# Low parts last in the divided sixth product, its block copies in layer one's last product, row statistics behind weight loads

## The chip, the cores and the metric

The kernel runs on one core of a Trainium2 chip. The metric is device time in microseconds (us) from the start of the launch to its end. Engines are named as the profile names them: PE is the matrix engine (TensorE; PEld are its weight loads), DVE is VectorE, ACT is ScalarE, POOL is GpSimd, SP is the sync engine, which only issues transfers. Transfers (DMAs) are issued from two queues: SP's (hardware, q1) and POOL's (software, q0).

## The reference

Two identical layers, each an attention without softmax and then a gated block that mixes over the sequence. Sequence S = 2048, width D = 512, 32 heads of 16, F = 1792, FH = 896. All is float32.

```python
x = x + A(layernorm(x));  x = x + B(layernorm(x));  x = x + A(layernorm(x));  x = x + B(layernorm(x))

def A(x):                      # phi(t) = (t + 1 if t > 0 else exp(t)) + 1e-6
    q, k, v = split_heads(x @ wqkv)
    kv, z = sum_s phi(k) v,  sum_s phi(k)
    return merge_heads(phi(q) kv / (phi(q) z + 1e-6)) @ wo

def B(x):
    z = gelu(x @ w_in)                        # [S, 1792]
    z1, z2 = z[:, :896], layernorm(z[:, 896:])
    g = w_sp @ z2 + b_sp[:, None]             # [S, S] x [S, 896]
    return (z1 * g) @ w_out
```

## The kernel before

Every matrix product in float32 is made from three products of rounded parts: an operand is split in a high part `h` (a copy by ACT) and a low part `l` (what is left, a subtraction by DVE), and PE adds h·h, h·l and l·h in one bank. So each tile of a weight costs one ACT pass, one DVE pass and three matmuls of 512 columns.

The program is written out in order for each engine; tile pools fix which buffer a tile gets and semaphores what it waits for. Within an engine's queue nothing overtakes, so the order of rows is the order of issue.

Each layer runs four stages. **P1** goes over the 16 row tiles of x (steps s = 1 to 18): layer norm, a transpose by way of DRAM (`xt`, loaded back by SP and turned by DVE at L448), the K and Q products, phi, and sums over K. In it SP also loads the weights of later stages, and `FSums` sums and splits parts of `w_in`. **The transition** forms the key-value state. **P2** makes the attention's output and z = gelu(x w_in); in layer two, `epair` makes z for two row tiles at a time by a seven-product scheme, and the row statistics of z are made from sums: `e3m` the mean on POOL, then a square with a running sum on ACT (L1084), then three POOL operations (L1086 to L1088) that give the factors with which `e4` normalises. `tail` is P2's last piece: `T[5]`, `T[6]`, `T[7]`, `T[4]` are its products with weights `w1s` and `w` which `wfetch` loads into pages through POOL (L205); `fmul` (L1145 to L1147) makes their matmuls.

**P4** multiplies by w_sp, also with seven products of block sums, in the order P2, P1, P6, P7, P4, P5, P3; a product has 8 steps k. Some of the seven are divided once more into seven products r of two steps each (`DIVIDED`: P2 and P4 in layer one, P2, P4 and P5 in layer two; the sixth product in this order is P5). Before a step's matmuls SP loads the step's raw block (`fetch1`), and `wsp` splits it: high part on ACT (L1678), low part on DVE (L1681). Some low parts (`KEPT`: P7, and of P5 the steps r = 1, 2, 4) are stored in DRAM by SP in layer one (`lowP7`, `lowP5`, L1686), and layer two loads them through POOL (L1684) instead of making them again. `mm_div` makes the 12 matmuls of a divided step through `acc` (L1889 h·high, L1890 h·low, L1891 l·high), `evac_div` adds the finished banks into the result's units, `gate` multiplies by z1.

The divided products need sums of two blocks of w_sp (or of `s1`, the block sums that layer one stores). They are built in DRAM by `halve(n)`: the first pieces are plain copies by SP (L1551), the others accumulating transfers by POOL (L1555), which add a second block into the copy; each moves 512 KB. `PARTS` says in which step of layer one's P4 which piece n runs, and a line in P1 runs the rest in layer two. The eight copies for P5 are n = 16 to 23, its eight adds n = 24 to 31.

Of the kernel before, what the change touches and what calls it, by code (L numbers as in the profile page):

```python
# [15 lines left out]
P = 128  # L16
# [3 lines left out]
NT = S // P  # L20
# [76 lines left out]
KEPT = ("P7", "P5")  # L97
# [13 lines left out]
FILL = {7: 3, 9: 3, 11: 3, 13: 3, 15: 3}  # L111
WADD = {2: 0, 4: 1, 6: 2}
PARTS = {("P1", 4 + k): k for k in range(4)} | {("P6", k): 4 + k for k in range(8)}
PARTS |= {("P7", k): 12 + k for k in range(4)}
LEFT = 4
SPN = 3
LOAD2 = (9, 10, 11, 14)
# [35 lines left out]
def mixer_kernel(ctx: ExitStack, tc: tile.TileContext, x_in, wqkv, wo_d, win1_d, win2_d, wsp_d, bsp_d, wout_d,  # L153
                 ident_d, mask_d, out_d):
    nc = tc.nc
# [7 lines left out]
    pages = Slots(main, "pg", 22)  # L163
    quads = Slots(main, "qd", 6)
# [288 lines left out]
    class P1:  # L453
# [185 lines left out]
        def run(self, sums):  # L639
            side = deque([self.win2] * NF)  # L640
            ND = NT - DEFER
            for s in range(1, NT + 2):
                for i in self.ahead(s, LEAD - 1, 3):
                    self.loadx(i)
                for i in self.ahead(s, LEAD + 1, 1):
                    self.turn.load(i)
                if 2 <= s < NT:
                    self.T_high(s)
                if s == 1:
                    if not self.kb:  # L650
                        self.K(0)
                    self.K(1)
                elif 2 < s <= NT:
                    self.K(s - 1)
                for i in self.ahead(s, LEAD, 2):
                    self.ln_a(i)
                if 2 <= s < NT:
                    self.T_low(s)
                if s <= NT:
                    self.K_phi(s - 1)  # L660
                if s <= ND:
                    self.Q(s - 1)
                if s == NT + 1:
                    self.late()
                if s <= NT:
                    self.xsplit(s - 1)
                    self.K_split(s - 1)
                for i in self.ahead(s, LEAD, 2):
                    self.ln_b(i)
                if s <= ND:  # L670
                    self.Q_phi(s - 1)
                if s >= 2:
                    self.Gmm(s - 2)
                if s == NT + 1:
                    self.late_phi()
                if self.L == 0:
                    if s == 2:
                        sums.slots = Sheets(bigs, 2)
                    if 2 <= s < 10:
                        sums.tick(s < 9)  # L680
                    if s == 10:
                        sums.store()
                    sums.store2()
                    if s in LOAD2:
                        sums.load2(pages if s > 12 else sums.slots)
                if s == 11:
                    self.wv = quads.get([P, 4, 512])
                    nc.sync.dma_start(self.wv, wqkv[:, 1024:1536].rearrange("(c p) f -> p c f", p=P))
                if s == 14:
                    self.wo = quads.get([P, 4, 512])  # L690
                    nc.sync.dma_start(self.wo, wo_d.rearrange("(c p) f -> p c f", p=P))
                if s in range(3,NT-1):
                    self.turn.pre(s + 1)
                if self.L == 0:
                    sums.add2(1, POOL2.get(s, 0))
                    sums.add2(0, DVE2.get(s, 0))
                if self.L:
                    if s > 1:
                        sums.halve(14 + s, None)
                    if s in WADD:  # L700
                        if not WADD[s]:
                            self.fsums = FSums()
                        self.fsums.load(WADD[s])
                    if s - 1 in WADD:
                        self.fsums.sums(WADD[s - 1])
                    if s - 2 in WADD:
                        self.fsums.split(WADD[s - 2])
                        if WADD[s - 2] == 2:
                            self.fsums.close()
                    if s <= 4:  # L710
                        self.win2.load(2)
                    else:
                        self.win2.piece()
                    if s == NT - 1:
                        self.win2.sums()
                    if s == NT:
                        self.win2.last()
                    continue
                if s > 3 and side:
                    side.popleft().piece()  # L720
                if s > 2 and side:
                    side[0].fetch()
# [104 lines left out]
    class P2:  # L827
# [167 lines left out]
        def epair(self, i, *between):  # L995

            V, A = nc.vector, nc.scalar.activation
            todo = deque(between)
            z = [ztag(i + k, [P, FH], f"z{self.L}") for k in range(2)]
            lo, hi = slice(0, HF), slice(HF, FH)  # L1000
            z0, z1 = ((t[:, lo], t[:, hi]) for t in z)

            def gelu(o, b):
                k, j = (o is not z0[0] and o is not z0[1]) * 1, (o is z0[1] or o is z1[1]) * 1
                self.mark = A(o, b, AF.Gelu_apprx_tanh, accum_out=self.acc(i + k)[:, j:j + 1])

            def other():
                if todo:
                    todo.popleft()()

            u = banks.get([P, HF])
            self.emul(i, 1, u, True, False)
            y = banks.get([P, HF])
            A(y, u, AF.Copy)
            v = banks.get([P, HF])
            self.emul(i, 5, v, True, True)
            c = z1[1]
            A(c, v, AF.Copy)
            banks.put(v)
            self.fout()  # L1020
            self.emul(i, 6, y, False, False)
            d = banks.get([P, HF])
            A(d, y, AF.Copy)
            V.tensor_add(y, y, c)
            other()
            self.emul(i, 2, u, False, True)
            gelu(z0[0], u)
            banks.put(u)
            self.emul(i, 7, d, False, False)
            V.tensor_add(c, d, c)  # L1030
            other()
            self.emul(i, 3, y, False, True)
            gelu(z0[1], y)
            banks.put(y)
            other()
            self.emul(i, 4, d, False, True)
            gelu(z1[0], d)
            gelu(z1[1], c)
            banks.put(d)
            pages.put(self.S.pop(i)[0][1])  # L1040
            while todo:
                other()
            self.e3m(i)
            self.e3m(i + 1)

        def e(self, i):
            n, k = divmod(i, 4)
# [25 lines left out]
                a = self.zacc[i] if a is None else a  # L1073
                nc.gpsimd.tensor_scalar(a[:, 2:3], a[:, 0:1], a[:, 1:2], -1.0 / FH, op0=OP.add, op1=OP.mult)

        def e3(self, i):
            if not self.L:
                self.zms[i] = stats(ztile[i], 2)
                return
            a = self.zacc.pop(i)  # L1080
            self.e3m(i, a)
            nm, v, rs, nb = (a[:, k:k + 1] for k in range(2, 6))
            t = pages.get([P, FH], mybir.dt.bfloat16)
            nc.scalar.activation(t, ztile[i], AF.Square, bias=nm, accum_out=v)  # L1084
            pages.put(t)
            nc.gpsimd.tensor_scalar(rs, v, 1.0 / FH, LN_EPS, op0=OP.mult, op1=OP.add)  # L1086
            nc.gpsimd.tensor_tensor(rs, rs, mhalf, op=OP.pow)
            nc.gpsimd.tensor_scalar(nb, nm, rs, None, op0=OP.mult)  # L1088
            self.zms[i] = None, rs, nb
# [111 lines left out]
        def tail(self):  # L1201
            V, A = nc.vector, nc.scalar.activation
            h, l = (t.bitcast(F32) for t in self.xT[3])
# [17 lines left out]
            for f in range(3):  # L1221
                ws.append(self.ws.popleft())
                v = banks.get(PAGE)
# [5 lines left out]
            for f in range(3):  # L1229
                y = self.y[f]  # L1230
                self.fmul(y, [t[:, 256:512] for t in ws[f]], self.T[6], False, False)
                pages.put(*ws[f])
                self.wfetch()
                d.append(banks.whole(PAGE))
                A(d[f], y, AF.Copy)
                V.tensor_add(y, y, c[f])
# [15 lines left out]
            x = [t[:, 2:4] for t in self.xT[3]]  # L1252
# [8 lines left out]
            for i in (NT - 2, NT - 1):  # L1261
                _, rs, nb = self.zms.pop(i)
                V.tensor_scalar(ztile[i], ztile[i], rs, nb, op0=OP.mult, op1=OP.add)
            for f in range(3):
                w = self.ws.popleft()
# [120 lines left out]
        def run2(self):  # L1386
            late = self.p1
            for s in range(1, NT + 3):
# [19 lines left out]
                else:  # L1408
# [44 lines left out]
                    if pair:  # L1453
# [22 lines left out]
                        elif s > NT:  # L1476
# [6 lines left out]
                            def late3():  # L1483
                                self.raw(1)
                                quads.put(*self.xT.pop(2))
                                self.T2()
                                self.e3(NT - 4)
                                self.e3(NT - 3)

                            self.epair(s - 4, late4, late3)  # L1490
                        else:
# [119 lines left out]
    class P4:  # L1611
# [79 lines left out]

        def kept(self, g):
            p, k = self.steps[g]
            if p not in KEPT or p == "P3" and k > 4:
                return None
            if p not in self.div:
                t = self.sums.lows[p][:, k]
# [104 lines left out]
        def mm_div(self, g, p, m):  # L1802
# [3 lines left out]
            name = "F" if r in (5, 3) else "X" if r in (1, 2) else "Y"  # L1806
            if q == 0 and r in (1, 5):
                self.bank[name] = [banks.get(PAGE) for _ in range(2)]
            if q == 0 and r == 6:
                pass  # L1810
            for i in range(2):
                for f in range(2):
                    self.acc(self.bank[name][f], h[:, i], l[:, i], slice(f * P, (f + 1) * P), w, i,
# [565 lines left out]
```

## Time and profile before

| | us |
|---|---|
| median of 3 runs | 1353.09 (1351.85 to 1355.10) |
| profiled execution | 1351.78 |
| its span | 1350.0 |
| PE busy | 1340.0 |
| DVE busy | 1037.7 |
| ACT busy | 726.3 |
| POOL busy | 463.8 |

The granted clock was 1.000 over the span. Rows of the timeline give start, duration, engine, line, operation, output and inputs, and in brackets the idle time before the row and what ended it. The names are those of the program: `pg`, `qd`, `bg` are pages of 512, 2048 and 3584 floats a partition, `bank` is a PE accumulator. A matmul's duration there is longer than the distance to the next, since they are pipelined: what counts is the distance from start to start. Layer two's P1 lies from about 680 to 815 us, its P2 to 1015, its P4 behind that.

### The profile page before, as it was taken

To read this page: it belongs to the slowest core of one execution; us is meant where nothing else is said; L and a number is where in the kernel's file an instruction comes from. 1 tells how busy PE (TensorE), PEld (TensorE's weight loads), DVE (VectorE), ACT (ScalarE), POOL (GpSimd) and SP (SyncE) were. 2 spreads that over 40 slices of the span, in tenths; PEclk is the share of its full clock that TensorE was granted. 3 is DMA by queue.
4 is the path that set the end of the run, shared out by engine and by line. 5 is a ranking of instruction groups with operands and counts; after the bars stand their busy time and mean duration, and the time that the engine had idled before them with its cause. 6 is when DMAs were issued, how large, how long until landed. Compare 5 with 4: busy or idle time off the path is not lost.

```text
span 1350.0 us, 19217 instructions
## 1 busy us (share of the span) xinstructions
PE 1340.0 (99%) x6540; PEld 1141.3 (85%) x6540; DVE 1037.7 (77%) x1658; ACT 726.3 (54%) x1219; POOL 463.8 (34%) x613
## 2 busy tenths in 40 slices
PE   9999999999999999999999999999999999999998
PEld 7888888888888888889988888888888888877898
DVE  7679877763797689897866877777689757889885
ACT  5774544334643255445667755556687333656454
POOL 3765765544122300301435453545450023022021
PEclk9999999999999999999999999999999999999999
DMA  5898477878877996843678783678767447479343
GB/s 183 277 311 281 164 264 252 289 262 263 296 241 266 299 292 208 291 164 64 152 192 287 208 199 94 204 249 252 235 195 252 143 171 264 155 242 315 106 78 64
DMA packets 174515, 294.50 MB, mean 218 GB/s; under 512 B 14544, under 2 KB 53968, under 8 KB 174160
## 3 DMA queue, kind: packets, MB, share of 16 engines
q1 hardware_dynamic: 155280, 253.67, 55.9%
q0 software_dynamic: 19136, 39.59, 13.4%
q8 instruction: 51, 0.84, 0.2%
q14 instruction: 48, 0.39, 0.1%
HBM read 206.18 MB, written 103.81 MB: 230 GB/s over the span
## 4 chain that ended last, share of the span: by engine, by line
PE 86%; DVE 4%; DMA 4%; issue 3%; ACT 1%; POOL 1%; SPq 0%; DVEq 0%; POOLq 0%; ACTq 0%
PE bank L1890 12%; PE bank L1891 12%; PE bank L1889 12%; PE bank L230 11%; PE bank L228 11%; PE bank L229 11%; PE bank L2087 3%; PE bank L2088 3%; PE bank L2089 3%; DMA qd<-lowP 1%; PE bank L988 1%; PE bank L987 1%; PE bank L986 1%; DMA pg<-xt 1%; PE bank L2101 1%
## 5 line engine op out<-in xcount | busy, mean ns | idle before, releaser
L1890 PE MATMUL bank<-qd,pg 128*128 128x512 f32 x760 | 296.1, 390 | 2.5 <-DMA qd<-lowP 1.7
L1889 PE MATMUL bank<-qd,pg 128*128 128x512 f32 x760 | 295.7, 389 | 0.0
L1891 PE MATMUL bank<-qd,pg 128*128 128x512 f32 x760 | 295.7, 389 | 0.0
L1678 ACT ACTIVATE qd<-qd 128x1024 fp32r<-128x1024 f32 x142 | 149.6, 1054 | 143.0 <-PE bank L1891 115.5
L1681 DVE TENSOR_TENSOR qd<-qd,qd 128x1024 fp32r<-128x1024 f32 x128 | 162.1, 1268 | 60.4 <-ACT qd L1678 60.4
L230 PE MATMUL bank<-qd,pg 128*128 128x512 f32 x448 | 174.8, 390 | 0.0
L1890 PEld LDWEIGHTS bank<-qd,pg 128*128 128x128 f32 x760 | 142.7, 188 | 33.3 <-DMA qd<-lowP 2.8
L1889 PEld LDWEIGHTS bank<-qd,pg 128*128 128x128 f32 x760 | 142.7, 188 | 29.7 <-ACT qd L1678 0.2
L1891 PEld LDWEIGHTS bank<-qd,pg 128*128 128x128 f32 x760 | 142.7, 188 | 29.5
L1930 POOL TENSOR_TENSOR bg<-bg,pg 128x512 f32<-128x512 f32 x28 | 47.9, 1710 | 213.6 <-DVE bg L1944 99.6
L228 PE MATMUL bank<-qd,pg 128*128 128x512 f32 x308 | 120.3, 391 | 0.3 <-DVE pg L217 0.3
L229 PE MATMUL bank<-qd,pg 128*128 128x512 f32 x308 | 120.0, 390 | 0.0
L230 PEld LDWEIGHTS bank<-qd,pg 128*128 128x128 f32 x448 | 84.1, 188 | 18.6 <-DVE pg L217 1.0
L363 POOL TENSOR_SCALAR rs<-mv 128x1 f32<-128x1 f32 x80 | 24.6, 308 | 197.4 <-DVE mv L361 188.0
L372 ACT ACTIVATE pg<-pg,nb,rs 128x512 f32<-128x512 f32 x52 | 42.1, 812 | 85.0 <-POOL nb L366 78.6
L1587 POOL TENSOR_TENSOR pg<-pg,pg 128x512 f32<-128x512 f32 x48 | 67.4, 1403 | 58.4 <-DMA pg<-in_wsp_dram 56.5
L214 ACT ACTIVATE pg<-pg 128x512 fp32r<-128x512 f32 x85 | 53.0, 624 | 63.1 <-DVE pg L448 18.2
L2089 PE MATMUL bank<-wo,qd 128*128 128x256 f32 x288 | 81.4, 283 | 0.0
L2087 PE MATMUL bank<-wo,qd 128*128 128x256 f32 x276 | 78.1, 283 | 0.0
L2088 PE MATMUL bank<-wo,qd 128*128 128x256 f32 x276 | 78.0, 283 | 0.0
L228 PEld LDWEIGHTS bank<-qd,pg 128*128 128x128 f32 x308 | 57.8, 188 | 12.6 <-DVE pg L217 0.7
L229 PEld LDWEIGHTS bank<-qd,pg 128*128 128x128 f32 x308 | 57.8, 188 | 12.1 <-DVE qd L217 0.3
(270 smaller groups left out, 3242.2 us busy)
## 6 DMA issues: line engine op xcount, KB each, us to landing
qd<-s SPq DMA_DIRECT2D x62, 512.0 KB, 4.3
qd<-in_wsp_dram SPq DMA_DIRECT2D x40, 512.0 KB, 4.0
qd<-hP SPq DMA_DIRECT2D x40, 512.0 KB, 4.6
pg<-z SPq DMA_DIRECT2D x56, 256.0 KB, 3.9
pg<-in_wsp_dram SPq DMA_DIRECT2D x52, 256.0 KB, 4.3
s<-pg SPq DMA_DIRECT2D x48, 256.0 KB, 3.7
z<-pg SPq DMA_DIRECT2D x40, 256.0 KB, 3.1
pg<-w POOLq DMA_DIRECT2D x38, 256.0 KB, 4.6
```

The lines of the kernel that those rows point to most:

```text
L228: nc.tensor.matmul(out, ah, bh, start=start, stop=False)
L229: nc.tensor.matmul(out, ah, bl, start=False, stop=False)
L230: nc.tensor.matmul(out, al, bh, start=False, stop=stop)
L1587: nc.gpsimd.tensor_tensor(t, a, b, op=OP.add)
L1678: self.mark = nc.scalar.activation(w[:, 0], r, AF.Copy)
L1681: nc.vector.tensor_sub(w[:, 1], r, w[:, 0].bitcast(F32))
L1889: m(out, h[:, o], w[:, 0, j, :], start=start, stop=False, skip_group_check=True)
L1890: m(out, h[:, o], w[:, 1, j, :], start=False, stop=False, skip_group_check=True)
L1891: m(out, l[:, o], w[:, 0, j, :], start=False, stop=stop, skip_group_check=True)
L2087: m(out, A, x, start=start and f == 0, stop=False, skip_group_check=True)
L2088: m(out, A, y, start=False, stop=False, skip_group_check=True)
L2089: m(out, B, x, start=False, stop=stop and f == 2, skip_group_check=True)
```

## The change

Four edits. (1) In layer two, the steps of P5 whose low part is loaded make their eight matmuls with the high weight part first and the four with the loaded low part last; there are 12 as before. (2) The eight copies for P5 (n = 16 to 23) run in layer one's P3 (the last product) instead of in steps 2 to 9 of layer two's P1, and the adds (n = 24 to 31) run at P1's even steps 2 to 16 instead of at steps 10 to 17. (3) P7's steps 6 and 7 aren't kept: layer one doesn't store their low parts, layer two makes them on DVE. (The condition that stood there before, on P3, never applied.) (4) In the tail, the row statistics of tiles NT-4 and NT-3 (`e3r`) and the means of NT-2 and NT-1 (`e3m`) come later among the loads of `wfetch`; the squares stay where they were.

```diff
@@
-PARTS |= {("P7", k): 12 + k for k in range(4)}
+PARTS |= {("P7", k): 12 + k for k in range(4)} | {("P3", k): 16 + k for k in range(8)}
@@ P1, layer two
-                    if s > 1:
-                        sums.halve(14 + s, None)
+                    if s % 2 == 0:
+                        sums.halve(23 + s // 2, None)
@@ epair
-            self.e3m(i)
-            self.e3m(i + 1)
+            if i < NT - 2:
+                self.e3m(i)
+                self.e3m(i + 1)
@@
-        def e3(self, i):
+        def e3(self, i, rest=True):
...
-            a = self.zacc.pop(i)
+            a = self.zacc[i]
             self.e3m(i, a)
...
+            if rest:
+                self.e3r(i)
+
+        def e3r(self, i):
+
+            a = self.zacc.pop(i)
+            nm, v, rs, nb = (a[:, k:k + 1] for k in range(2, 6))
             nc.gpsimd.tensor_scalar(rs, v, 1.0 / FH, LN_EPS, op0=OP.mult, op1=OP.add)
@@ tail
                 self.fmul(y, [t[:, 256:512] for t in ws[f]], self.T[6], False, False)
                 pages.put(*ws[f])
                 self.wfetch()
+                if f == 0:
+                    self.e3m(NT - 2)
+                    self.e3m(NT - 1)
+                if f == 1:
+                    self.e3r(NT - 4)
+                    self.e3r(NT - 3)
@@ run2, late3
-                                self.e3(NT - 4)
-                                self.e3(NT - 3)
+                                self.e3(NT - 4, False)
+                                self.e3(NT - 3, False)
@@ kept
-            if p not in KEPT or p == "P3" and k > 4:
+            if p not in KEPT or p == "P7" and k > 5:
@@ mm_div
+            if self.L and self.kept(g) is not None:
+                M = nc.tensor.matmul
+                for x in range(2):
+                    for i in range(2):
+                        for f in range(2):
+                            o, b = slice(f * P, (f + 1) * P), self.bank[name][f]
+                            if x:
+                                M(b, h[:, i, o], w[:, 1, i, :], start=False, stop=r in (2, 4) and q == 1 and i == 1,
+                                  skip_group_check=True)
+                            else:
+                                M(b, h[:, i, o], w[:, 0, i, :], start=r == 1 and q == 0 and i == 0, stop=False,
+                                  skip_group_check=True)
+                                M(b, l[:, i, o], w[:, 0, i, :], start=False, stop=False, skip_group_check=True)
+                pages.put(h, l)
+                quads.put(w)
+                return
```

PE, the first step of P5 in layer two, before. `qd5_179` holds the step's weights, high and low, `pg0` the high part of z, `pg10` its low part; L1890 is the matmul with the loaded low part.

```order
L1889 MATMUL bank5_367_11948<-qd5_179_11897,pg0_1130_11851 128x512
L1890 MATMUL bank5_367_11948<-qd5_179_11897,pg0_1130_11851 128x512
L1891 MATMUL bank5_367_11948<-qd5_179_11897,pg10_1131_11852 128x512
L1889 MATMUL bank1_368_11949<-qd5_179_11897,pg0_1130_11851 128x512
L1890 MATMUL bank1_368_11949<-qd5_179_11897,pg0_1130_11851 128x512
L1891 MATMUL bank1_368_11949<-qd5_179_11897,pg10_1131_11852 128x512
```

The same step after, from its third pair on: L1833 and L1835 are the products with the high weight part, L1830 those with the loaded low part.

```order
L1833 MATMUL bank5_367_11946<-qd5_179_11895,pg0_1130_11849 128x512
L1835 MATMUL bank5_367_11946<-qd5_179_11895,pg10_1131_11850 128x512
L1833 MATMUL bank1_368_11947<-qd5_179_11895,pg0_1130_11849 128x512
L1835 MATMUL bank1_368_11947<-qd5_179_11895,pg10_1131_11850 128x512
L1830 MATMUL bank5_367_11946<-qd5_179_11895,pg0_1130_11849 128x512
L1830 MATMUL bank1_368_11947<-qd5_179_11895,pg0_1130_11849 128x512
```

The first matmul that reads the low part was the step's second and is its ninth.

POOL in layer two's tail, before, from the last two statistics of tile NT-3 on: `acc` are the sums and factors of a row tile, `w1s` and `w` the weights that `wfetch` loads.

```order
L1086 TENSOR_SCALAR acc<-acc 128x1
L1087 TENSOR_TENSOR acc<-acc,mhalf 128x1
L1088 TENSOR_SCALAR acc<-acc 128x1
L1074 TENSOR_SCALAR acc<-acc 128x1 x2
L205 DMA pg_981_10265<-w1s_1_0_119 128x512
L205 DMA pg_982_10267<-w1s_1_1_120 128x512
L205 DMA pg_984_10303<-w_3_0_101 128x256
L205 DMA pg_985_10305<-w_3_1_102 128x256
L205 DMA pg_986_10316<-w_4_0_103 128x256
L205 DMA pg_987_10318<-w_4_1_104 128x256
L205 DMA pg_988_10329<-w_5_0_105 128x256
L205 DMA pg_989_10331<-w_5_1_106 128x256
```

And after (L1075 is the mean, L1094 to L1096 are the statistics of NT-4):

```order
L205 DMA pg_981_10255<-w1s_1_0_119 128x512
L205 DMA pg_982_10257<-w1s_1_1_120 128x512
L205 DMA pg_984_10293<-w_3_0_101 128x256
L205 DMA pg_985_10295<-w_3_1_102 128x256
L1075 TENSOR_SCALAR acc<-acc 128x1 x2
L205 DMA pg_986_10308<-w_4_0_103 128x256
L205 DMA pg_987_10310<-w_4_1_104 128x256
L1094 TENSOR_SCALAR acc<-acc 128x1
L1095 TENSOR_TENSOR acc<-acc,mhalf 128x1
L1096 TENSOR_SCALAR acc<-acc 128x1
```

The same three rows for NT-3 follow, and only then `w_5_0_105` and `w_5_1_106`. The two `w1s` loads and the first two `w` loads moved ahead of all eight row operations; the last two `w` loads stand behind all of them.

SP in layer two's P1, step 2, before: `xt` is the transposed x, `hP` the piece for P5, `in_win` parts of w_in.

```order
L419 DMA xt_4_7071<-pg_667_7069 128x4x128
L1551 DMA hP_1_0_164<-s_145 16x8192
L734 DMA qd_108_7094<-in_win_dram 128x512 x2
L302 DMA bg_15_7021<-in_win_dram 128x512 x2
L196 DMA pg_668_7100<-x_5_84 128x512
L196 DMA pg_669_7102<-xt_4_7071 128x512
```

POOL in the same step, after: the add that takes the copy's step stands behind the sum over K (L542).

```order
L363 TENSOR_SCALAR rs<-mv 128x1
L364 TENSOR_TENSOR rs<-rs,mhalf 128x1
L366 TENSOR_SCALAR nb<-mv,rs 128x1
L542 TENSOR_TENSOR pg_652_6994<-pg_652_6994,pg_662_7049 128x512
L1569 DMA hP_1_0_164<-s_145 128x1024
```

The copy left SP's queue, and the add came into POOL's, at the even steps; at the odd steps nothing took the copy's place.

More of the change, by code (lines that the diff above doesn't have):

```diff
@@ L1808, in mm_div @@
                 self.bank[name] = [banks.get(PAGE) for _ in range(2)]
-            if q == 0 and r == 6:
-                pass
+            if self.L and self.kept(g) is not None:
[14 more added lines that the diff above has]
+                return
             for i in range(2):
```

## The prediction

> **What bounds the kernel now.** I read the page's busy shares first, then the table of what TensorE (PE) waited for, then the timeline around each of its waits.
>
> ```profile
> PE 1340.0 (99%) x6540; PEld 1141.3 (85%) x6540; DVE 1037.7 (77%) x1658; ACT 726.3 (54%) x1219; POOL 463.8 (34%) x613
> ...
> PE bank L617 <- DVE pg L612: 2.3, 1, 2.3
> PE bank L1890 <- DMA qd<-lowP: 1.7, 2, 0.9
> PE bank L1147 <- DMA pg<-w1s: 0.9, 1, 0.9
> PE bank L1890 <- DVE qd L1681: 0.8, 1, 0.8
> PE bank L228 <- DVE pg L217: 0.3, 1, 0.3
> ```
>
> PE is busy 1340.0 of 1350.0 us. The diff leaves every matmul in the program, so only PE's waits can move the end. The list is short. The first line is the program's start and stays. The second and third name the loads that this change makes less urgent or issues earlier. The last two are a weight split in layer one and a step of layer two's first stage (P1).
>
> ```profile
> 1203.29 0.39 PE L1891 MATMUL bank<-qd,pg 128*128 128x512 f32 x1
> 1203.52 0.39 PE L1889 MATMUL bank<-qd,pg 128*128 128x512 f32 x1
> 1204.82 0.50 PE L1890 MATMUL bank<-qd,pg 128*128 128x512 f32 x1 [0.91 <-DMA qd<-lowP]
> 1205.15 0.40 PE L1891 MATMUL bank<-qd,pg 128*128 128x512 f32 x1
> ...
> 1237.45 0.39 PE L1889 MATMUL bank<-qd,pg 128*128 128x512 f32 x1
> 1238.66 0.50 PE L1890 MATMUL bank<-qd,pg 128*128 128x512 f32 x1 [0.83 <-DMA qd<-lowP]
> ...
> 1005.35 0.39 PE L1146 MATMUL bank<-bg,pg 128*128 128x512 f32 x1
> 1006.60 0.50 PE L1147 MATMUL bank<-bg,pg 128*128 128x512 f32 x1 [0.86 <-DMA pg<-w1s]
> ...
> 755.14 0.39 PE L230 MATMUL bank<-pg,pg 128*128 128x512 f32 x1
> 755.78 0.50 PE L228 MATMUL bank<-qd,pg 128*128 128x512 f32 x1 [0.25 <-DVE pg L217]
> ```
>
> The reader should measure from start to start. Undisturbed matmuls start 0.23 us apart (1203.29 to 1203.52). At 1203.52 the next one comes 1.30 later, so 1.07 are lost; the one behind it comes 0.33 later, 0.10 more. The first wait on lowP thus costs 1.17, the second 0.98 + 0.10 = 1.08, the wait on w1s 1.02 + 0.10 = 1.12, the one at 755 0.41 + 0.10 = 0.51.
>
> **The sixth product's matmuls (mm_div).** Each of the 6 divided steps keeps its 12 matmuls. The loaded low part was an operand of the second; now it is one of the ninth. That is 7 x 0.227 = 1.59 us of grace, more than the 1.07 and 0.98 that the loads were late. The grace is lost if the load starts later too, so its issue matters:
>
> ```profile
> 1197.02 0.72 POOL L1684 DMA_DIRECT2D qd<-lowP  x1 [3.18 <-DMA qd<-hP]
> ...
> 1229.75 0.72 POOL L1684 DMA_DIRECT2D qd<-lowP  x1 [1.96 <-PE bank L1891]
> ```
>
> The second issue waits for a matmul that frees its buffer, the first for the raw block of the same buffer chain. Both move with PE and don't lag behind it, and the 1.59 hold in relation to PE. Margins of 0.5 and 0.6 us stay. Gain: 1.17 + 1.08 = 2.25; bounds 1.1 (one load again too late) and 2.3. The price is that the bank's last value for the first half comes 2 matmuls (0.45) later for the evacuation on DVE, on which PE doesn't wait in the list above.
>
> **The row statistics in the tail.** On POOL six statistics and two means stood ahead of eight weight loads:
>
> ```profile
> 992.97 0.73 POOL L1086 TENSOR_SCALAR acc<-acc 128x1 f32<-128x1 f32 x1 [2.78 <-ACT pg L1084]
> ...
> 998.78 1.43 POOL L1074 TENSOR_SCALAR acc<-acc 128x1 f32<-128x1 f32 x2
> 1000.15 1.18 POOL L205 DMA_DIRECT2D pg<-w1s  x2
> ...
> 1005.31 0.19 POOL L1086 TENSOR_SCALAR acc<-acc 128x1 f32<-128x1 f32 x1 [0.75 <-ACT pg L1084]
> 1005.58 0.57 POOL L1087 TENSOR_TENSOR acc<-acc,mhalf 128x1 f32<-128x1 f32 x1
> 1006.25 0.30 POOL L1088 TENSOR_SCALAR acc<-acc 128x1 f32<-128x1 f32 x1
> ```
>
> The last load that PE wants at 1005.35 went out at 1000.77 and landed at 1006.56, 5.8 later. With nothing ahead but a page that comes free about 994 (with the second of the squares, of which the row at 992.97 waited for the first), it goes out some 6 us earlier and lands near 1000. The 1.12 go. What is late next are the loads w_105 and w_106, now behind the six statistics:
>
> ```profile
> 998.63 1.29 DVE L1216 TENSOR_TENSOR qd<-qd,pg 128x512 f32<-128x512 f32 x2
> ...
> 1014.48 0.39 PE L1145 MATMUL bank<-bg,pg 128*128 128x512 f32 x1
> ...
> DMA to landing us min/median/max: 2.9/5.0/9.7
> ```
>
> The load w_101 can't go before its page is read at 999.93 (the end of the DVE row). Two loads, two means (1.43) and two loads follow, 0.55 each: 1003.6. Then come six statistics, 2 x (0.19 + 0.57 + 0.30 and gaps) = 2.6 at the fast price, 5.8 at the price of 992.97 to 998.78. So w_105 starts at 1006.2 to 1009.4, and with the tile's median landing (the last row) is there at 1011.2 to 1014.4. PE wants it at 1014.48, by then 1.12 earlier: 1013.36. From 2.2 early to 1.0 late. I take 0, since the DVE work beside POOL after 1003 is that of the fast rows. Gain of the part 1.12; bounds 0.1 and 1.12. The means and statistics themselves are read over 4 us later.
>
> On the length of such a load the Trainium skill, "DMA: Bandwidth & Descriptors", section "Anatomy of one DMA — SWDGE (gpsimd) path", fits 2.0 us plus bytes by 436 GB/s. For 256 KB that is an estimate of 2.6 us, by which w_105 could not be late in any case; the row above has a minimum of 2.9 and a median of 5.0, so the trace decides for the longer one.
>
> **The block copies and adds.** Eight 512 KB copies leave the SP queue of layer two's P1 for layer one's last product. There DMA has room, and PE's operands there were over 4 us early:
>
> ```profile
> 587.00:594.00 7.00, 7.00 (x33) 5.79 (x32) 6.97 (x13) 4.32 (x8) 0.00 (x0) 1.00 0.71 246
> ```
>
> Cost there 0 (the DMA share, next to last, is 0.71 in the fullest of four such windows); if that cover were gone, a copy costs what it does below. In P1 the copies of steps 2 to 9 go, and accumulating adds, which lay at steps 10 to 17, take steps 2, 4, 6 and 8, with the rest at even steps to 16. Their price:
>
> ```profile
> q1 hardware_dynamic: 155280, 253.67, 55.9%
> q0 software_dynamic: 19136, 39.59, 13.4%
> ...
> 730.00:745.00 15.00, 15.00 (x68) 12.43 (x67) 10.87 (x18) 11.38 (x22) 7.20 (x10) 1.00 0.87 293
> ...
> 742.40 0.73 DVE L448 STREAM_TRANSPOSE bank<-pg 128x512 f32<-128x512 f32 x1 [1.17 <-DMA pg<-xt]
> ...
> 747.49 0.63 ACT L535 ACTIVATE pg<-pg 128x512 fp32r<-128x512 f32 x1 [2.05 <-DVE pg L524]
> ...
> 750.71 0.69 DVE L524 SCALAR_TENSOR_TENSOR z_q<-bank,z_q 128x512 f32<-128x512 f32 x1 [1.86 <-ACT z_q L521]
> ```
>
> From the queues' shares, SP's transfers cost 0.559 x 1350 / 253.67 = 2.97 us a MB, 1.56 for 512 KB; POOL's 4.57 a MB, 2.40. An add for a copy is 0.84 us more of a full burst in each even step, and one copy less in each odd step, where the engines come to rest anyway. At step 6 that decides: the load of xt that VectorE waits for at 742.40 ends such a burst, and from there DVE, ACT (747.49) and DVE (750.71) hand on without slack to the wait at 755. So 0.84 later there is 0.84 later on PE. At step 2 and 4 PE is over 2 us ahead. The adds' issue on POOL (0.9 each) lies in idle time of 3 to 5 us. I take +0.85: the price of the nearest rows. Bounds: -0.5 (the adds don't delay xt, and the wait at 755 goes too) and +1.7 (step 8 pays as well).
>
> A rule speaks against this part: the Trainium skill, "DMA: Bandwidth & Descriptors", section "Issuing engines are not separate DMA queues", says that transfers started by POOL and SP run on the same 16 engines and interleave, so POOL's queue is no way around SP's burst. By that rule the part is a loss as taken here; if the queues were independent it would be 0 to -0.5, and the sum 0.85 to 1.35 lower (rival 1). The share of 0.87 in a window with both agrees with the rule.
>
> **Product P7's two low parts.** Layer one drops two 512 KB stores, layer two drops two loads of POOL and splits on DVE instead:
>
> ```profile
> L1681 DVE TENSOR_TENSOR qd<-qd,qd x128: 1209/1221/2334, 340.9 to 1260.5; 128x1024 fp32r<-128x1024 f32 x128
> ...
> 1140.00:1160.00 20.00, 20.00 (x89) 16.54 (x89) 13.48 (x30) 8.92 (x14) 1.43 (x2) 1.00 0.73 238
> ...
> 499.61 3.67 DVE L1949 TENSOR_TENSOR bg<-pg,bank 128x512 f32<-128x512 f32 x6
> ```
>
> Two splits of 1.22 us lie on a DVE that is busy 13.48 of 20 there. The first also waits for ACT, which holds the DVE queue about 3 us; what stands behind is used 7 us later. Cost 0, and if that cover were gone up to 2. In layer one the wait of 0.8 on L1681 ends a run of DVE work (six evacuations, 3.67 us) whose first weight landed ahead of the stores: -0.05, with -1.0 as the end.
>
> **Sum.** -2.25 - 1.12 - 0.05 + 0.85 = -2.6. Against the profiled execution (1351.78, span 1350.0 and 1.8 around it) 1349.2; that execution was 1.31 below the median of three, 1353.09, from which I forecast 1350.5. No change within 0.2% is 1350.4 to 1355.8 here, about what a measurement of this kernel can tell.
>
> **The rivals.** (1) The adds are hidden, or layer one's wait goes as well. For it: the odd steps lose a copy, and two stores leave SP's queue. Against it: the full burst at 742.40, and the DVE run at 499.61. Time: 1353.09 - 3.4 - 0.5 to -1.0 = 1348.7 to 1349.2.
>
> (2) The grace isn't enough in one place: one lowP load late by another 0.6, or w_105 behind slow statistics. Then 1.0 to 1.2 come back: 1351.5 to 1351.7. For it the longest landing of 9.7; against it the margins above. If the reordering did nothing at all, both lowP waits would stay: 1352.7.
>
> (3) Slower: the adds jam the first half of P1. Landing times, for the adds and then for the copies, were:
>
> ```profile
> DMA to landing us min/median/max: 5.0/8.3/9.6
> ...
> DMA to landing us min/median/max: 4.0/5.6/10.1
> ```
>
> If an add delays xt not by 0.84 but by the 2.7 us between those medians, steps 6 and 8 each pay 2.7, step 4 the 0.6 above its 2.1 of slack: +6.0, the sum +2.6, 1355.7. From 2.8 us an add on, it is slower by over 0.2%; at 4 us it is 2 x 4 + 1.9 - 3.4 = +6.5, 1359.6. For it: adds read and write what copies only write. Against it: in all of POOL's traffic 512 KB took 2.40 us.
>
> **How the numbers follow.** Forecast 0.40 (own range 1349.8 to 1351.4, half of it faster by over 0.2%); rival 1 0.25; rival 2 0.20; rival 3 0.15, of which 0.13 beyond +0.2%. Faster: 0.20 + 0.25 = 0.45. Slower 0.13. Same: 0.20 + 0.20 + 0.02 = 0.42. The range, 1348.4 to 1354.6, leaves the far part of rival 3 and the low end of rival 1 with layer one's wait in full.
>
> **What would show it.** In the profile after, PE's waits should have no line for lowP and none for w1s, and matmuls around the old 1203, 1237 and 1005 should start 0.23 apart. The wait on L217 in P1 should grow from 0.3 to about 1.1, with VectorE's idle time before L448 (xt) up by 0.8. The two statistics rows behind the means should end before w_105 is wanted. I am wrong if P1's waits grow by over 2 us, if lowP keeps a line, or if a new line for w appears.

## The result, and the profile after

The change makes the kernel slower. The median went from 1351.85 us (11 runs) to 1356.58 (11 runs); the ratio is 1.0036, 95% interval 1.0025 to 1.0047, so +4.9 us. The forecast was 1350.5, and 1356.58 lies above the range's end of 1354.6.

The table of what PE waited for, of the kernel after (engine, line, what ended the wait: us in total, times, longest):

```profile
PE bank L228 <- DVE pg L217: 4.9, 2, 2.5
PE bank L617 <- DVE pg L612: 2.3, 1, 2.3
PE bank L228 <- ACT qd L214: 1.5, 1, 1.5
PE bank L1918 <- DVE qd L1695: 0.8, 1, 0.8
PE bank L1830 <- DMA qd<-lowP: 0.4, 1, 0.4
PE bank L230 <- DVE pg L217: 0.2, 1, 0.2
```

Against the list of before: the wait on w1s in the tail is gone, of the 1.7 on lowP 0.4 are left, and the 0.3 in P1 (L217) have become 4.9. The third line is at 283 us, in layer one, ahead of everything that the change touches; so it is not of the change, but of this execution (1358.38 us, 1.8 above its median).

P1's two large waits in the timeline of the kernel after:

```profile
733.60 0.39 PE L230 MATMUL bank<-pg,pg 128*128 128x512 f32 x1
736.33 0.50 PE L228 MATMUL bank<-qd,pg 128*128 128x512 f32 x1 [2.34 <-DVE pg L217]
736.66 0.40 PE L229 MATMUL bank<-qd,pg 128*128 128x512 f32 x1
...
752.83 0.39 PE L230 MATMUL bank<-pg,pg 128*128 128x512 f32 x1
755.76 0.79 PE L228 MATMUL bank<-qd,pg 128*128 128x512 f32 x1 [2.54 <-DVE pg L217]
756.35 0.63 PE L229 MATMUL bank<-qd,pg 128*128 128x512 f32 x1
756.78 0.63 PE L230 MATMUL bank<-qd,pg 128*128 128x512 f32 x1
```

Start to start, with 0.227 for an undisturbed matmul, the first costs 2.50 + 0.11, the second 2.70. Behind the second the matmuls come 0.43 apart, not 0.23: the granted clock was 0.50 there (the row is in the last section), and the stretch cost another 1.5. With three small waits on L217 and L214 (744, 779 and 785: 0.9 in all) P1 lost 7.7 us, against 0.8 before.

What was late is the turned x. VectorE's waits for it (L448), of the kernel before and of the kernel after:

```profile
708.98 0.73 DVE L448 STREAM_TRANSPOSE bank<-pg 128x512 f32<-128x512 f32 x1 [1.15 <-DMA pg<-xt]
725.71 0.73 DVE L448 STREAM_TRANSPOSE bank<-pg 128x512 f32<-128x512 f32 x1 [2.42 <-DMA pg<-xt]
```

```profile
713.52 0.73 DVE L448 STREAM_TRANSPOSE bank<-pg 128x512 f32<-128x512 f32 x1 [2.74 <-DMA pg<-xt]
733.17 0.73 DVE L448 STREAM_TRANSPOSE bank<-pg 128x512 f32<-128x512 f32 x1 [5.35 <-DMA pg<-xt]
751.81 0.73 DVE L448 STREAM_TRANSPOSE bank<-pg 128x512 f32<-128x512 f32 x1 [3.08 <-DMA pg<-xt]
```

At steps 2, 4 and 6 the wait grew from 1.15, 2.42 and 1.17 to 2.74, 5.35 and 3.08: 1.6, 2.9 and 1.9 more. The first two add up to 4.5; PE's lead of 2.1 at step 4 leaves 2.4, close to the 2.50 at 733.

PE's wait at 753 is for step 6's own operand, which a split on VectorE (L217) makes out of the turned x. That split in the kernel before and in the kernel after:

```profile
746.18 0.67 DVE L217 TENSOR_TENSOR pg<-bank,pg 128x512 fp32r<-128x512 f32 x1
```

```profile
755.03 0.67 DVE L217 TENSOR_TENSOR pg<-bank,pg 128x512 fp32r<-128x512 f32 x1
```

Before, it was ready 0.3 ahead of the matmul that reads it (747.21). After, it started 8.85 later, while PE was only 5.8 behind its old place: 2.9 from ahead of P1 (the same matmul starts at 678.61 and at 681.55), 2.6 from the wait at 733, and the rest from the small wait at 744. 8.85 - 5.8 - 0.3 leave the 2.7 of the wait. It is not the old wait at 755: that one is a step later, and PE no longer waits at its matmul (765 after).

Why it was late stands in the DMA view of the kernel after, over step 4 (718 to 735 us, 40 slices of 0.43 us: busy tenths of the 16 DMA engines, GB/s, then each queue's packets, MB and share):

```profile
DMA  0004987999328697989759999999999997544104
GB/s 0 0 0 123 290 194 275 400 371 328 82 72 173 140 173 135 183 125 159 125 130 260 313 357 337 376 419 405 390 405 377 376 351 284 169 146 153 58 0 39
...
q1 hardware_dynamic: 2504, 3.16, 53.2%
q0 software_dynamic: 144, 0.52, 23.7%
```

q0 moved one add here, 0.52 MB in 23.7% of 17 us: 4.03 us of all 16 engines, not the 2.40 that I had taken. For nearly 4 us the engines are 50 to over 90% busy but move only 125 to 185 GB/s, where they moved 330 to 400 shortly before and 310 to 420 behind it.

### The profile page after: what moved, and what is told of

Read it like the earlier page. It is cut to its first block, busy times and chain, and to the rows that moved or that the text cites. A ratio compares the mean times of both kernels' runs of the same rounds, so it can differ in the third digit from the quotient of the medians.

```text
span 1356.6 us, 19206 instructions
## 1 busy us (share of the span) xinstructions
PE 1342.7 (99%) x6540; PEld 1141.6 (84%) x6540; DVE 1040.0 (77%) x1660; ACT 726.4 (54%) x1219; POOL 461.1 (34%) x611
## 4 chain that ended last, share of the span: by engine, by line
PE 89%; DMA 4%; DVE 2%; ACT 1%; POOL 1%; issue 1%; SPq 1%; DVEq 0%; POOLq 0%; ACTq 0%
PE bank L1918 12%; PE bank L1919 12%; PE bank L1917 12%; PE bank L230 11%; PE bank L228 11%; PE bank L229 11%; PE bank L2115 3%; PE bank L2116 3%; PE bank L2117 3%; DMA pg<-xt 1%; PE bank L986 1%; PE bank L988 1%; PE bank L987 1%; PE bank L384 1%; PE bank L1155 1%
## 5 line engine op out<-in xcount | busy, mean ns | idle before, releaser
L1918 PE MATMUL bank<-qd,pg 128*128 128x512 f32 x736 | 286.5, 389 | 0.8 <-DVE qd L1695 0.8
L1917 PE MATMUL bank<-qd,pg 128*128 128x512 f32 x736 | 286.4, 389 | 0.0
L1919 PE MATMUL bank<-qd,pg 128*128 128x512 f32 x736 | 286.3, 389 | 0.0
L1695 DVE TENSOR_TENSOR qd<-qd,qd 128x1024 fp32r<-128x1024 f32 x130 | 165.7, 1276 | 54.4 <-ACT qd L1692 54.4
L230 PE MATMUL bank<-qd,pg 128*128 128x512 f32 x448 | 175.5, 392 | 0.2 <-DVE pg L217 0.2
L1918 PEld LDWEIGHTS bank<-qd,pg 128*128 128x128 f32 x736 | 138.1, 188 | 30.1 <-DVE qd L1695 1.2
L1917 PEld LDWEIGHTS bank<-qd,pg 128*128 128x128 f32 x736 | 138.1, 188 | 28.9 <-ACT qd L1692 0.2
L1919 PEld LDWEIGHTS bank<-qd,pg 128*128 128x128 f32 x736 | 138.1, 188 | 28.4
L228 PE MATMUL bank<-qd,pg 128*128 128x512 f32 x308 | 121.5, 394 | 5.0 <-DVE pg L217 4.9
L229 PE MATMUL bank<-qd,pg 128*128 128x512 f32 x308 | 120.6, 391 | 0.0
L230 PEld LDWEIGHTS bank<-qd,pg 128*128 128x128 f32 x448 | 84.4, 188 | 19.3 <-DVE pg L217 1.4
L214 ACT ACTIVATE pg<-pg 128x512 fp32r<-128x512 f32 x85 | 53.0, 624 | 69.7 <-DVE pg L448 23.9
L228 PEld LDWEIGHTS bank<-qd,pg 128*128 128x128 f32 x308 | 58.2, 189 | 18.9 <-DVE pg L217 6.8
L229 PEld LDWEIGHTS bank<-qd,pg 128*128 128x128 f32 x308 | 58.2, 189 | 12.1 <-DVE qd L217 0.3
```

Of the source, the lines that this page charges most:

```text
L228: nc.tensor.matmul(out, ah, bh, start=start, stop=False)
L229: nc.tensor.matmul(out, ah, bl, start=False, stop=False)
L230: nc.tensor.matmul(out, al, bh, start=False, stop=stop)
L1695: nc.vector.tensor_sub(w[:, 1], r, w[:, 0].bitcast(F32))
L1917: m(out, h[:, o], w[:, 0, j, :], start=start, stop=False, skip_group_check=True)
L1918: m(out, h[:, o], w[:, 1, j, :], start=False, stop=False, skip_group_check=True)
```

## The experiments

Theory 1: an accumulating transfer is dear, 4.0 us of the engines against about 1.5 for a plain copy, and in the bursts of the even steps it holds up the xt loads of SP; all of the loss comes from there. Theory 2: it is not the accumulating, but any transfer of that size from POOL's queue in that place. Theory 3: the loss comes from the copies in layer one or from another part. Ratios are to runs of the kernel before on the same chip, each with its 95% interval.

**Everything but the copies and adds.** The edit, from the changed kernel:

```diff
-PARTS |= {("P7", k): 12 + k for k in range(4)} | {("P3", k): 16 + k for k in range(8)}
+PARTS |= {("P7", k): 12 + k for k in range(4)}
-                    if s % 2 == 0:
-                        sums.halve(23 + s // 2, None)
+                    if s > 1:
+                        sums.halve(14 + s, None)
```

> The change without its part on the block copies and adds (these stand as before); low parts last, kept steps and statistics as changed. Theory 1 (the adds among the even steps' bursts of layer two's P1 cost all of the loss, some 7 us): before is 1351.9, minus 1.1 (the wait on w1s) and minus 1.6 to 2.3 (the waits on lowP): 1348.5 to 1349.2, P1's waits as before, 0.8 in all. Theory 3 (the loss comes from another part, or from layer one): 1354 or more.

Measured: 1348.51 us, ratio 0.9976 (0.9967 to 0.9986), -3.2 us. Theory 3 falls as far as it means the other parts. P1 lost at most 0.1 us in this run's profile, not the 0.8 of before, and 0 to 0.3 in those of the last three experiments below, whose copies and adds stand as before, so the 0.8 are of one execution.

**The copies and adds alone.** The same four lines the other way, in the kernel before.

> Only the copies and adds are moved as in the change. Theory 1: P1's waits grow from 0.8 to 7.9, before + 7.1: 1357.5 to 1360, slower than the whole change by what the other parts give. Theory 3: 1351 to 1353.

Measured: 1359.62 us, ratio 1.0053 (1.0039 to 1.0067), +7.2. P1 lost 7.2 us in its profile. So this part costs 7 to 8 us (from the change's 1.0036 and the 0.9976 above: 8.1), the others gain 3.

**Copies in layer one, adds late as before.** From the changed kernel:

```diff
-                    if s % 2 == 0:
-                        sums.halve(23 + s // 2, None)
+                    if s > 9:
+                        sums.halve(14 + s, None)
```

> The change, but with the eight adds at steps 10 to 17 of layer two's P1, where they stood before; the copies stay in layer one's last product. Theory 1: the copies cost nothing in layer one, and without them steps 2 to 9 have room: P1's waits at 755 and 775 shrink from 0.8 to 0 to 0.3, in all 1347.7 to 1349. If moving the copies is what costs (theory 3), 1354 or more.

Measured: 1349.02 us, ratio 0.9977 (0.9969 to 0.9986). The copies cost nothing in layer one; what costs is where the adds went. PE has no wait in P1, and VectorE waits 2.5 us for xt in the whole run (6.6 before, 13.7 after).

**Adds at odd steps.** From the changed kernel:

```diff
-                    if s % 2 == 0:
-                        sums.halve(23 + s // 2, None)
+                    if s % 2 == 1 and s > 1:
+                        sums.halve(23 + (s - 1) // 2, None)
```

> The change, but with the eight adds at the odd steps 3 to 17 instead of the even steps 2 to 16. Theory 1 with the collision as its cause: at odd steps SP loads only two or three tiles and its engines come to rest, so an add of 4 us finds room, P1's waits stay under 1 us: 1348 to 1349.5. If an add delays the turned x wherever it stands in the first half: 1353 or more.

Measured: 1347.74 us, ratio 0.9969 (0.9958 to 0.9981), -4.2 us: faster than both kernels. The same adds in the same stage, one step later, cost nothing. PE's waits in this run, first lines, and VectorE's waits for xt:

```profile
PE bank L617 <- DVE pg L612: 2.3, 1, 2.3
PE bank L1918 <- DVE qd L1695: 1.1, 2, 0.8
PE bank L1917 <- ACT qd L1692: 0.3, 1, 0.3
```

```profile
715.93 0.73 DVE L448 STREAM_TRANSPOSE bank<-pg 128x512 f32<-128x512 f32 x1 [0.16 <-DMA pg<-xt]
724.03 0.73 DVE L448 STREAM_TRANSPOSE bank<-pg 128x512 f32<-128x512 f32 x1 [0.63 <-DMA pg<-xt]
```

What differs is the add's place. POOL issues that of step 5 at 722.65, behind the loads of step 4's burst; in the changed kernel it issues that of step 4 at 719.90, ahead of the four loads of `w1s`. The add itself stays dear. From 720 to 732 us of this run:

```profile
q0 software_dynamic: 144, 0.52, 26.5%
```

That is 3.18 us of the engines, against 4.03 in the burst.

**Plain copies in the adds' place.** The second block isn't added. From the changed kernel:

```diff
-                d = nc.gpsimd.dma_start(self.halves[p, m, q], src, accum_op=OP.add, max_dma_last_dim=4096)
+                if n < 24:
+                    d = nc.gpsimd.dma_start(self.halves[p, m, q], src, accum_op=OP.add, max_dma_last_dim=4096)
+                else:
+                    d = nc.gpsimd.dma_start(self.halves[p, m, q], src, max_dma_last_dim=4096)
```

> The changed kernel, but the eight transfers at even steps are plain copies by POOL of the same 512 KB instead of accumulating ones: the second block isn't added into the sums for P5, the computation lacks that. Theory 1 (the price of accumulating: 4.0 us of the 16 engines against some 1.6): xt is late by no more than before, P1's waits 0 to 1, 1348.5 to 1350. Theory 2 (any transfer from POOL's queue in that place holds up SP's): P1's waits stay near 7, 1355.5 to 1357.

Measured: 1349.41 us, ratio 0.9980 (0.9971 to 0.9989). The DMA view over its step 4 (717 to 734 us):

```profile
q1 hardware_dynamic: 2640, 3.41, 60.3%
q0 software_dynamic: 144, 0.52, 9.0%
```

The same 144 packets and bytes from the same queue take 9.0% of 17 us, 1.53 us, and PE loses 1.1 us in P1, 0.7 of them in one wait on L217. VectorE waited 1.27, 2.37 and 1.94 us for xt at steps 2, 4 and 6, against 1.15, 2.42 and 1.17 before:

```profile
745.78 0.73 DVE L448 STREAM_TRANSPOSE bank<-pg 128x512 f32<-128x512 f32 x1 [1.94 <-DMA pg<-xt]
```

Theory 2 falls as the cause of the loss: it is the accumulating. At step 6 a plain copy from POOL's queue still goes with 0.8 of the delay of 1.9; whether its place causes that isn't tested.

**Longer rows.** In the changed kernel each add moves 64 rows of 8 KB instead of 128 of 4 KB:

```diff
-accum_op=OP.add, max_dma_last_dim=4096)
+accum_op=OP.add, max_dma_last_dim=4096 if n < 24 else 8192)
```

> The changed kernel, adds at even steps as there, but each add moves 64 rows of 8 KB instead of 128 of 4 KB. If the price of an add goes by bytes: 4.0 us of the 16 engines as before, P1's waits near 7, 1355.5 to 1357. If it goes by packets: near 2 to 2.5 us, P1's waits 0 to 2, 1348.5 to 1350.5.

Measured: 1357.39 us, ratio 1.0045 (1.0033 to 1.0058). Its queue row over step 4 (718 to 735 us):

```profile
q0 software_dynamic: 80, 0.52, 23.9%
```

80 packets instead of 144 take 4.06 us: the price doesn't go by packets. P1 lost 9.8 us in this run's profile, 2.9 of them at half clock (last section).

**Adds in two halves.** From the changed kernel, one half of each add at the even step, the other at the odd one behind it:

```diff
-                    if s % 2 == 0:
-                        sums.halve(23 + s // 2, None)
+                    if s > 1:
+                        sums.halve(23 + s // 2, None, s % 2)
...
+                dst = self.halves[p, m, q]
+                if part is not None:
+                    dst, src = dst[part:part + 1], src[part:part + 1]
```

> The changed kernel, but each add is cut in two of 256 KB, one at the even step and one at the odd step behind it. Theory 1 with a price by bytes: 2.0 us in each even burst, against the copy's 1.5 before: P1's waits 0.5 to 1.5, 1348.3 to 1350. If an add has a large fixed price whatever its size: P1's waits 4 to 7, 1353 to 1356.5.

Measured: 1350.18 us, ratio 0.9983 (0.9972 to 0.9995), -2.3 us. With half the dose in the burst the waits of L448 are 0.74, 2.87 and 1.23, those of before within 0.5, and P1 loses 1.1 us in all. One half add stands in the DMA view from 713 to 721.5 us:

```profile
q0 software_dynamic: 80, 0.26, 22.2%
```

22.2% of 8.5 us are 1.89, for 256 KB with the 80 packets that took 4.06 for 512 KB. So the price goes by bytes, and there is no large fixed one.

**One add in a burst.** The adds at odd steps, with one of the eight moved to step 4, or to step 6:

```diff
-                    if s % 2 == 0:
-                        sums.halve(23 + s // 2, None)
+                    if s in PIECE:
+                        sums.halve(PIECE[s], None)
+PIECE = {3: 24, 4: 25, 7: 26, 9: 27, 11: 28, 13: 29, 15: 30, 17: 31}    # step 4
+PIECE = {3: 24, 5: 25, 6: 26, 9: 27, 11: 28, 13: 29, 15: 30, 17: 31}    # step 6
```

> The changed kernel with the adds at odd steps, but one of them at even step 4 in place of step 5. Theory 1 (each add in an even step's burst makes that step's turned x late by itself): a wait of PE of 0.7 to 2.6 near 733, in all 1348.4 to 1350.4. If the loss needs several adds in a row, a single one is taken up by the slack: 1347.5 to 1348.2.

> The same with the one add at step 6 in place of step 7. Theory 1: there is no slack at step 6 (before, its turned x already led to the wait at 755), so VectorE's idle time before it grows by 1.9 to 2.5 and PE waits 2 to 2.7 near 750, with up to 1.5 more if the clock drops behind the wait: 1349.8 to 1352. If several adds are needed: 1347.5 to 1348.2.

Measured: 1351.54 us, ratio 1.0000 (0.9990 to 1.0011), and 1350.15, ratio 0.9993 (0.9984 to 1.0001). VectorE's wait in the burst, in the first kernel and in the second:

```profile
728.75 0.73 DVE L449 STREAM_TRANSPOSE bank<-pg 128x512 f32<-128x512 f32 x1 [3.71 <-DMA pg<-xt]
```

```profile
743.66 0.73 DVE L449 STREAM_TRANSPOSE bank<-pg 128x512 f32<-128x512 f32 x1 [3.31 <-DMA pg<-xt]
```

A single add delays its own step's xt by 3 us (0.63 at step 4 and none at step 6 with all adds at odd steps), as theory 1 says. Where it shows on PE I had wrong: the add at step 4 makes no wait near 733; VectorE carries the delay on, and PE waits 1.66 at 756. The add at step 6 costs PE 1.2 in P1, not 2 or more, because without copies and adds in the bursts before it there is slack at step 6. Against the kernel with odd steps alone the two lose 3.1 and 2.4 per mille, 4.2 and 3.2 us; PE's waits in P1 account for 2.0 and 1.2. In the profiled executions, 4.4 and 2.3 us apart from that of odd steps alone, 1.9 and 0.6 arise ahead of layer two's P1, where the three programs are the same, and 0.3 to 0.4 behind it. Whether that holds for the medians isn't settled; the intervals are about 1 per mille wide on each side.

**The other parts, one by one**, each in the kernel before: the order of matmuls in `mm_div` alone, the statistics (`e3`, `e3r`, `epair`, `tail`) alone, and the one line in `kept` alone, each as in the diff of the change.

> Only the order of matmuls in the divided sixth product is changed. If both lowP waits go: before minus 2.25. If one stays in part, as in the profile after (0.55 and the restart): minus 1.6. If the load drifts later with the earlier matmuls: 0 to minus 0.6.

> Only the row statistics and means in layer two's tail are moved behind weight loads. The wait on w1s goes: before minus 1.1. If w_105 is then late: 0 to minus 0.5, and a new wait on w in the tail.

> Only the two low parts of product P7 are no longer stored and loaded again. As forecast: minus 0.05, within 0.3 of before. The rival: layer one's wait at 505 goes too, minus 1.1. If the two splits on DVE show: plus 0.5 to plus 2.

Measured: 1349.42 us, ratio 0.9985 (0.9975 to 0.9995), -2.0; 1351.16, ratio 0.9993 (0.9982 to 1.0004), -0.9, not clear of noise; 1351.47, ratio 1.0001 (0.9991 to 1.0010). PE's waits with the reordered matmuls alone, and then with the statistics alone:

```profile
PE bank L617 <- DVE pg L612: 2.3, 1, 2.3
PE bank L1904 <- DVE qd L1681: 0.8, 1, 0.8
PE bank L1147 <- DMA pg<-w1s: 0.6, 1, 0.6
```

```profile
...
PE bank L1904 <- DMA qd<-lowP: 1.5, 2, 0.9
PE bank L1903 <- ACT qd L1692: 0.9, 1, 0.9
PE bank L1904 <- DVE qd L1695: 0.8, 1, 0.8
PE bank L1153 <- ACT bank L1170: 0.3, 1, 0.3
```

The first has no wait on lowP at all, the second none on w1s and none on w. A new wait of 0.3 behind an ACT copy (L1170) in the tail, at 981, takes 0.6 of the second's gain in that execution; the kernel with adds in two halves shows it too (0.4), the changed kernel doesn't. The second's waits on L1903 and, behind L1695, on L1904 are in layer one (506 and 508), ahead of what its edit touches.

## Why the prediction was wrong

**The block copies and adds** were the step that failed: "I take +0.85: the price of the nearest rows". The runs put it at 7.2 (alone) to 8.1 (the change against the change without it). P1's loss grew by 6.9 us, where the prediction called itself wrong from 2 on. The mechanism was the one named, an add in a full burst that makes xt late at the head of a chain without slack; its price was mis-sized. I took 2.40 us for an add from the mean over POOL's queue, which mixes adds with plain loads. An add in a burst takes 4.03, a plain copy from the same queue 1.53. The difference in a burst is thus 2.5, not 0.84. The trace of before could have told: its DMA view from 788 to 798 us, where nearly all the traffic is adds, and from 764 to 774, with one add:

```profile
q0 software_dynamic: 388, 1.46, 77.4%
```

```profile
q0 software_dynamic: 144, 0.52, 33.3%
```

That is 7.74 us for 1.46 MB, 2.78 for 512 KB, and 3.33 with some traffic beside it. The bound that I gave, +1.7, came from the same mean. Of the loss in P1, 1.5 us are the half clock behind the second wait, for which the sum has no term.

**The slack at step 4** ("at step 2 and 4 PE is over 2 us ahead") was read rightly, but as if each step had it anew. The delays of steps 2 and 4 added up to 4.5 and went through it. The path at step 6 was incomplete, too: I followed the late xt to the wait at 755, but a delay of more than 0.3 stops PE first at step 6's own operand, at 747.

**Rival 3** had the mechanism and, by landing times, a price of 2.7 an add; it gave 1355.7, within 0.9 of the median of 1356.58, with a chance of 0.15. What I set against it, that 512 KB of POOL's traffic took 2.40, was the mean again. That the number came so near is partly luck: it charged steps 6 and 8 with 2.7 each and step 4 with 0.6, while in the profile steps 4 and 6 cost 2.6 and 2.7, the half clock 1.5, and all that came later 0.7.

**The rule on the engines.** The Trainium skill, "DMA: Bandwidth & Descriptors", section "Issuing engines are not separate DMA queues", agrees with the runs in that POOL's add and SP's loads got in each other's way: with an add of 4.03 us in the burst VectorE waited 2.9 longer for xt at step 4, with a plain copy of 1.53 from the same queue no longer than before (2.37, before 2.42). The share of 0.87 that I set beside the rule shows nothing of it: from 730 to 745 us of the kernel before only SP's queue moved the data (86.7% of the engines), and the first add of P1 goes out at 766.

**The sixth product**: -2.25 forecast, -2.0 measured alone, both waits gone. In the changed kernel one load is still late, by 0.55 more than the grace of 1.59 (at 1230), so lowP kept a line, one of the signs of being wrong. The same step's load had made no wait in the profile of before, but one of 2.65 in the run with the kept parts alone, and the wait that was 1.07 at 1203 was 1.97 in the run with the copies and adds alone: the landings vary from execution to execution by more than the grace, which one profile couldn't show. Of the ten profiles with the reordered matmuls five keep one wait on lowP, of 0.5 to 1.2. So "the 1.59 hold in relation to PE" was wrong as a certainty; rival 2 had it. **The statistics**: -1.12 forecast, -0.9 measured, not clear of noise, the wait on w1s gone and no wait on w_105. The loads w_105 and w_106 move 128 KB each, not the 256 KB for which I estimated; the six of that size took 6.4 us from issue to landing in the median of the kernel before, longer than the 5.0 that I took, and still PE had no wait on them after. **The kept parts**: -0.05 forecast, +0.1 measured; the wait at 505 was 0.4 in its profile (0.8 before and in the kernel after), and the time doesn't show it. Together -3.4 forecast, -3.2 measured.

## What to carry to other kernels

Price a transfer by its kind, in a window of the trace where it stands alone; the mean of a queue hides the dear kind. Before moving one, ask which load ends the burst that it enters, and who waits for that load: the same eight adds cost 7 to 8 us at even steps and nothing at odd ones. Slack along a chain is spent once, so delays of successive steps are to be added before it is taken off.

## What was not expected of the hardware

An accumulating DRAM transfer of 512 KB took 4.03 us of the 16 DMA engines beside other traffic, a plain one from the same queue 1.53, with the same 144 packets; the price stayed with 80 longer packets (4.06) and went down with the bytes (1.89 for 256 KB).

After a wait PE's clock can fall to half. Windows of the kernel after (us, busy times with counts of PE, PEld, DVE, ACT and POOL, then granted clock, DMA share and GB/s), and below it of the kernel with longer rows:

```profile
752.60:755.60 3.00, 0.62 (x3) 0.19 (x1) 2.93 (x6) 2.20 (x4) 1.00 (x3) 0.95 0.29 89
755.60:758.70 3.10, 2.94 (x7) 2.36 (x8) 1.99 (x4) 2.37 (x4) 2.09 (x5) 0.50 0.02 6
758.70:762.00 3.30, 3.30 (x15) 2.72 (x15) 2.45 (x6) 3.11 (x8) 1.23 (x2) 1.00 0.91 208
```

```profile
732.90:736.50 3.60, 0.39 (x2) 0.00 (x0) 2.98 (x5) 2.22 (x4) 0.25 (x2) 0.90 0.37 99
736.50:742.40 5.90, 5.76 (x14) 4.51 (x15) 4.43 (x10) 5.07 (x12) 3.42 (x4) 0.50 0.46 142
```

After the wait of 2.7 us the clock was 0.50 for 3 us, which cost 1.5; after one of 3.5 us it was 0.50 for nearly 6, which cost 2.9. It doesn't go by the wait's length alone: in the kernel with copies and adds alone a wait of 1.97 at 1213 was followed by half clock (first row), and in the kernel with the kept parts alone a wait of 2.65 at 1218 was not (the other rows):

```profile
1215.50:1219.50 4.00, 4.00 (x12) 3.16 (x11) 1.54 (x4) 0.58 (x1) 0.00 (x0) 0.57 0.58 215
```

```profile
1217.90 0.39 PE L1889 MATMUL bank<-qd,pg 128*128 128x512 f32 x1
1220.78 0.50 PE L1890 MATMUL bank<-qd,pg 128*128 128x512 f32 x1 [2.49 <-DMA qd<-lowP]
1221.11 0.39 PE L1891 MATMUL bank<-qd,pg 128*128 128x512 f32 x1
```

The Trainium skill, "TensorE: Matmul & The Clock Gate", section "What's actually happening", says that the array's clock is set from its recent activity in free-running windows of 3.4 us. That a wait's length alone doesn't decide fits with it; where the windows lie no run here shows. The table in that section of the Trainium skill names an idle window of about 3.4 us for the fall to half clock; here a wait of 1.97 us was enough, and the measurement decides.
